# Grouped state products, a parametric ReLU for the sign of the weights, and a one-level last product in a cross-attention and SERF kernel

## The chip, the cores and the metric

The kernel runs on one core of one Trainium2 chip. The metric is the device time of one execution in microseconds. The engines are TensorE (PE in the profile, with its weight loads as PEld), VectorE (DVE), ScalarE (ACT), GpSimd (POOL) and SyncE (SP), which issues most of the DMAs. Each engine works off its own list of instructions in order.

## The reference, cut to what matters

Two blocks follow each other. The first is attention between the tokens `x` of a batch row (8 rows, 8 heads, 512 tokens, 64 columns) and a small state (32 rows a head); the second is a layer with the activation `h * erf(softplus(h))`.

```python
scores = x @ state^T / 8            # per batch row and head
a = exp(scores - max);  a /= sum + 1e-9
xread = a @ state                   # 512 tokens
a2 = the same over state @ x^T / 8
sread = a2 @ x                      # 32 state rows
x2 = concatenate([xread, sread]) with the heads side by side   # 8 * 544 rows of 512
h = x2 @ w_in                       # 512 -> 2048
g = h * erf(softplus(h))
out = g @ w_out                     # 2048 -> 512, 4352 rows in all
```

The weights are handed over as 64-bit floating-point numbers. The kernel computes in 32 bits.

## The kernel before, in words

**Passes and units.** The 2048 hidden columns are worked off in two passes of 1024, since the weights of one pass are what stays on the chip. A unit is one batch row in one pass: unit 0 of the first pass is written out by hand (`first_unit`), units A1 to A7 are the other rows of the first pass, SA and SB are the state rows of both passes, B0 to B7 are the rows of the second pass, whose results are added to what the first pass stored.

**A unit's steps.** `attention` makes the weights `a`, turned, in `y`. `mixed` multiplies a row's state matrices with `w_in` (a 32-row block for each head, on 64 rows of the array), so that the hidden values are `a` times that product; the four blocks X11, X12, X21, X22 and three sums of them (M1 to M4) lie in `m`. `hidden` then forms the product with seven block products instead of eight (the Strassen-Winograd way), in two halves `f0` and `f1`; `chain` spells out the order of the seven and of the copies between them, on banks 0, 1 and 2 of the accumulation memory. Softplus (`soft`), Erf (steps `e0`, `e1`) and the multiplication (`g0`, `g1`) follow on ScalarE and VectorE, in one of two buffers `ring`. `sums_a` prepares the four sums for the second product.

**The second product.** In the first pass and for SA and SB it is `second`: seven products of the one level, steps `p1` to `p7`, in banks 3 to 5, whose results are stored. In the second pass it is `second_twice`: each of the seven is again made of seven (`inner`, with sums of the activations made by `inner_sums` and of the weights made by `twice`). `twice` overwrites the corner `w12` of each of the seven weight blocks with `w22 - w12` (steps t03 to t63). The last unit, B7, has its own form, `second_last`: it reads back what the first pass stored (steps l0 to l3), adds the products to it and stores the sum; two groups of four and two of the seven go through `inner`, and the seventh (S4) is taken at one level, for which `saved` keeps the one corner that it needs.

**Reading the weights.** `piece` turns 1024 64-bit numbers a partition into 32-bit ones, with i0 to i7 for `w_in` and o0 to o7 for `w_out` (i0 in two parts, so there are seventeen): `a0` on ScalarE scales the high words, `a1` on ScalarE scales the low words, `v0` on VectorE shifts the first result left by 3 bits, `v1` adds the low part, `v2` copies the sign bit from the high word. In the profile `a0` is L344, `a1` L346, `v0` L348, `v1` L350, `v2` L351.

**The order.** Nothing is left to a scheduler: `ORDER` is a list of the steps' names, written out, and every engine gets its instructions in that order. A name such as `~7*11` is eleven products of the identity, whose result nobody reads. `issue` calls each step; `in_order` forbids any other order.

**Lines of helpers.** Adds, subtractions and multiplications all have the lines of `add` (L223), `sub` (L224) and `mul` (L225); copies and the DVE's transposes have L231. L575 is a product of `mixed`, L623 of `hidden`, L675 of `second`, L734 of `inner`, L815 and L819 of the last unit's S4 (256 and 128 columns), L854, L865 and L886 of unit 0, L468 the read `sread` of a row, L612 Softplus, L631 Erf, L926 a product of the state units.

In the profile a product is two rows of MATMUL, a transpose one.

Of the kernel before, what the change touches and what calls it, by code (L numbers as in the profile page):

```python
# [8 lines left out]
F32 = mybir.dt.float32  # L9
# [8 lines left out]
lx0 warm lst0 lx1 lx2 lx3 i0l0 lst6 lst3 lst5 lst2 ~7*11 x0 lst4 lst8 s0 lst7 x1 s0c lst1 x0c i1l0  # L18
x3 x1c i1l1 i0l1 q0 x3c i2l1 x2 q00c i2l0 q01c i3l0 x2c tm0 i3l1 i0a0 big0 q1 i0a1 max0 q11c i0v0
q10c less0 ~7*4 tm1 i0v1 u0 exp0 max1 i0v2 u1 less1 o0l0 n00 sum0 exp1 big1 sum1 i1a0 inv0 inv1  # L20
norm0 i1a1 big i1v0 ~6*13 ta0 norm1 i0+a1 i1v1 ~7*1 ta1 i0+a0 wt0 n00c1 i1v2 n00c0 wt1 ta1c i0+v0
~4*6 n02 ta0c i0+v1 n02c0 i2a0 i0+v2 n02c1 o0l1 ~7*5 n01 i2a1 h0 n01c1 a1xq2 i2v0 n01c0 i2v1 a1xq7
h1 wz a1xq6 h0s i2v2 i3a0 a1xq3 u1c ~7*1 n10 i3a1 i3v0 h2 a1xq1 n10c1 h0c i3v1 h1s a1xq4 n10c0 h3
h2s i3v2 a1xq0 h1c o0a0 y01 a1xq5 n12 wn1 o0a1 h4 y02 o1l0 n12c1 wn0 o1l1 h2c n12c0 u0c o2l0 tw1
h4c o0v0 h3s tw0 a1tx3 h3c o0v1 tw1c h5 tw0c h4s o0v2 rd0 a1tx0 h2e rn0 a1tx2 ~7*2 rt0 h7 rc0
a1tx1 h0e y04 h2g yl0 a1s o3l1 h0g a1x2 h5s h6 o2l1 a1c0 a1c1 o3l0 a1tu0 o1a1 i4l0 a1tu1 A1m0 i4l1
a1my0 h6s a1x3 o10 a1mx1 A1m01 a1my1 o1a0 a1mx0 o20 A1m00 a1ms o1v0 h5c a1sb0 h7c h7s o1v1 A1m1
o00 o1v2 a1ex0 A1m11 a1sb1 i5l1 A1m10 o02 a1sm0 a2xq7 a1ex1 A1M1 a1ey1 a1sm1 h6c o12 a1ey0 a1iz
a1nm0 a1ta0 o22 A1M2 h4e a1nm1 o2a1 A1f01 y11 a1ta1 A1f05 A1f0c y12 a1ty1 o2a0 A1f06 A1M3 A1f02
y13 A1f0u2 a1ty0 A1f07 y14 A1f0c11 a1kz o2v0 A1f11 i5l0 A1f0u3 A1M4 a1x0 i4a0 A1f0c22 A1f04 a1iy  # L30
h4g A1f03 A1f0c21 A1f1c o2v1 o3a1 A1f16 A1f0c12 A1f12 A1f1u2 i4v0 a1z3 i4a1 A1f15 a1x1 o2v2 a1z0
A1f17 o3a0 a1z2 i4v1 o24 a1z1 A1f1u3 i5a1 i4v2 A1f14 h6e o3v0 i4k o04 A1f1c22 i6l0 A1f1c11 o3v1
a2xq5 A1f1c21 A1f13 a2xq6 h6g rd1 A1f0s11 a2xq2 y03 A1f0s21 o3v2 o14 a2xq4 i5a0 rn10 rn11 i6l1 rt1
A1f1s11 o06 i5v0 A1f0s12 i5v1 A1f1s22 rc1 o16 o0c i5v2 A1f1s12 A1f1c12 o30 i5k a2tx3 a2xq3 A1f1s21
T1 A1f0s22 a2xq1 o32 a2tx2 a2xq0 T2 A1e1 o34 a2x0 T3 a2x3 a2x1 o36 A1g1 yl1 i6a0 i7l0 A1e0 o26
a2tx1 i6v0 o3c a2tx0 A1g0 a2s a2c1 a2c0 a2tu1 A1p10 o1c a2tu0 i6a1 o1d a2my0 a3xq3 o2c a2mx1 A2m0
A1A1 o3d A1p11 a3xq0 A2m01 a2mx0 A2m00 yk0 a2sb1 A2m1 i7l1 a2sb0 a3xq7 a2ex1 a2my1 A1p50 a2ex0
A1A2 a3xq6 A1pc A2m11 a2sm1 a3xq1 A1p60 A2m10 a2sm0 i6v1 A1p51 a2iz a2nm0 a2nm1 A1p61 a2ta0 i6v2
A2f01 A1pu2 a2ms y21 i6k a2ey0 A1p20 a2ta1 a3xq2 A2f0c A2M1 a2ey1 y22 A2M2 A2f02 a2ty0 A2f06
A2f0c11 a2ty1 A2f05 A2M3 A2f0u2 a2kz y23 A2f11 a2x2 A1A3 a3xq4 A2f07 i7a0 y24 A1p70 a3tx0 A2f0u3  # L40
i7v0 i7a1 A2f0c22 A2f04 A2M4 a2z0 a3tx3 A1p71 A2f0c21 a2z2 A1A4 A2f1c a2z3 a2z1 A2f16 a3tx1 a3xq5
i7v1 A2f03 A2f0s22 o0d A2f1u2 A2f12 i7v2 A1pu3 A2f17 A2f1c11 A2f0c12 o4l0 rd2 A2f1s11 a2iy A1pc22
A2f1u3 A2f0s12 A2f15 A1d3 rn21 rn20 A2f0s11 a3tx2 yl2 rt2 A2f14 A2f1c22 i7k rc2 A2f0s21 T4 yk2 a3s
A2f1c21 o2d A2f1s12 a3x3 A2f13 a3c1 yk1 A2f1s22 A1p21 a4xq0 A2f1c12 a3c0 a3tu1 A2f1s21 a3x1 a3tu0
A1p40 a4xq4 a3mx1 A2e0 a3x2 a3sb1 o4l1 A3m0 a3mx0 a3my1 A1p30 A3m01 A2g0 A3m00 A2e1 A3m1 a3my0
A1p41 A1pc11 A2g1 A1p31 a3ex1 A3m10 a3sb0 A3m11 A2A1 A2p10 a3ex0 A1pc21 a3sm0 a3sm1 A2p11 A1pc12
a3ms a3iz A1d1 a3ey0 a3nm0 A2p50 a4xq1 A2pc a3nm1 a3ey1 a3ta0 a3x0 A2p51 A2A2 a4xq5 a4xq6 y31
a3ta1 A3f01 o4a0 A3M1 A2p60 a3ty0 A3f0c A3M2 y32 A3f02 a3ty1 y33 A3f06 a3kz A3M4 a4xq7 A2p61 A3M3
A3f0u2 a3iy A3f0c11 A2A4 a4xq2 A3f07 A2pu2 y34 a4xq3 o4v0 o4a1 A3f05 A3f11 A3f0u3 a3z0 A3f0c22
A3f04 a3z3 a4tx2 a3z1 A3f03 A3f0s11 a3z2 A3f0c21 A2p20 A3f0c12 A3f1c o4v1 A3f0s12 A3f0s21 A3f16  # L50
A3f0s22 o4v2 A3f12 A3f1u2 A2A3 rd3 o4k A1d0 A3e0 A3f17 yl3 rn30 rn31 a4tx3 o5l1 rt3 A3f15 a4tx0
a4x2 a4tx1 A3f1u3 A2p70 A3f1c11 A3f1c22 rc3 A3g0 a4s A3f1s11 A3f14 a4c0 a5xq5 A3f1s22 A3f13 a4tu0
a4c1 a5xq2 a4mx0 A2p71 A3f1c21 A3f1c12 A3f1s12 A1d2 a4tu1 a5xq0 A3f1s21 A4m0 a4my0 A2pu3 a4x3
a4mx1 A2p21 o5l0 a4my1 a5xq1 A2pc22 A3e1 a4sb0 A2p40 a4x0 a4sb1 A2d3 A4m01 a4x1 A3g1 A2pc11 a5xq4
A2p30 A4m00 o6l0 A4m1 a4ms A3A1 a4ex1 a4ex0 A3p10 a4sm1 a4ey1 a4sm0 A4m10 A4m11 a4iz A2p41 a4nm0
a4ey0 a4ta0 A3p11 a4nm1 A2pc21 A4M1 o5a1 y41 a4ta1 A4f01 a4ty1 A2p31 A4f0c a4ty0 A3pc y42 o5a0
a4kz A4M2 A4f02 a5xq3 A3A2 A4f06 A4f0c11 A4M3 A3p60 A4f0u2 y43 a4iy y44 o5v0 A4f07 o5v1 A4f05
A4f0u3 a4z1 A4M4 a4z2 A4f11 A4f0c22 a4z0 A4f04 A2pc12 a4z3 a5xq6 a5tx1 A4f03 A4f0c21 a5tx0 A3p61
A4f1c a5xq7 a5tx2 A3A3 A2d1 rd4 A4f0s22 A4f0c12 A4f0s12 A4f16 rn41 a5x2 rn40 o5v2 o6l1 rt4 A4f15
A4f1u2 yk3 A4f0s21 a5tx3 A4f17 rc4 a5s A4f1u3 A3pu2 A4f1c22 A4f12 A4f0s11 a6xq1 a5c1 A4f14 a5c0  # L60
a5tu1 a5x1 A4f13 yl4 a5my1 a6xq2 A3p50 a5tu0 A4e0 a5mx1 a6xq3 a5sb1 A5m0 a5mx0 A2d2 A4f1c11 a5x3
a5my0 A3p70 A5m01 a6xq0 a5sb0 A5m00 a5ms A3A4 a5x0 A5m1 o5k a5ex1 a6xq6 A3p71 A4f1c21 a5sm1 a5ex0
a6xq7 A4f1c12 a5ey0 a5sm0 A3p20 A2d0 A5m10 a5iz a6xq5 a5ey1 a5nm0 o6a1 A3p51 a5ta0 y51 A5m11 a5nm1
A5f01 a5ta1 A3p21 A4f1s11 y52 A5M1 A5f0c A4f1s12 A5M2 A3pu3 A5f05 A5M3 A4f1s22 A5f06 a6tx1 a5ty1
A5f02 A5f0u2 a5ty0 A4f1s21 A3p40 A3pc22 a5kz A5f0c11 y53 a6xq4 a6tx0 A5f07 y54 yk4 A4g0 A4e1 A5f11
A3p30 A5f0u3 A4g1 A3pc11 A5f04 a5z0 A3p31 a5z3 A5f0s11 a5iy a5z1 A5M4 a5z2 A3p41 A5f0c22 a6tx2
A5f0c21 A4A1 A5f1c A5f03 A5f0s22 A5f16 a6tx3 o6a0 A3pc12 rd5 A5f1u2 A5f0c12 A3d1 A5f17 yl5 rn51
rn50 o6v0 rt5 A4p10 A5f1u3 A4A3 rc5 A5f0s21 A3pc21 o6v1 a6s A4A2 A5f15 a6c1 a7xq4 a6c0 A5f12
A5f0s12 a6x1 a6tu0 A6m0 a7xq3 a6mx0 a6tu1 A5f14 a6x2 A5e0 a6mx1 A3d3 A4p11 a7xq2 a6sb0 a6my1 A6m00
a7xq6 A4p50 A5f1c22 a6my0 o7l0 a6ex0 a6ms a7xq1 A4A4 A5f13 A4pc A6m01 yk5 A4p60 a6sb1 a7xq5 a6sm0  # L70
a6ex1 a6ey0 a6sm1 a7xq7 A4p61 A5f1c11 a6iz A5f1c21 a7xq0 a6nm0 a6ey1 A6m1 a6ta0 a6x0 A4pu2 a6nm1
A6f01 A6m10 y61 a6ta1 A6m11 A4p70 A6f0c A6M1 y63 a6ty0 A4p71 A6M2 y62 A5f1c12 A4p51 A4pu3 a6iy
# [93 lines left out]
def kernel(  # L166
# [140 lines left out]
    def load_st(h):  # L307
        i, e = h // 2, h % 2
        nc.sync.dma_start(out=st[Ns * i:Ns * i + Ns, 1:B, D * e:D * e + D],
                          in_=state[1:B, h].rearrange("b n d -> n b d"))  # L310

    def piece(kind, j):

        g = j + 4 * (kind == "o") if j < 4 else j
# [741 lines left out]
```

## Time and profile before

| | us |
|---|---|
| median of 3 runs | 714.45 |
| the profiled execution | 714.29 |
| its span, first to last instruction | 712.4 |
| matmuls by line: L675 / L623 / L734 in the chain | 27% / 26% / 24% of the span |
| VectorE, sign bit (L351), 17 operations | 19.6 |
| ScalarE, function table loads, 60 | 77.0 |
| granted TensorE clock | 0.998 |

How to read it: a group's line gives the source line, the engine, the operation, output and inputs, the shape, how often it ran, the busy time and the mean of one; then the idle time of the engine before these instructions and what ended it. In the timeline a line begins with the start and the duration in us. The chain is the work that ended last, followed back from the end.

### The profile page before, as it was taken

To read this page: it belongs to the slowest core of one execution; us is meant where nothing else is said; L and a number is where in the kernel's file an instruction comes from. 1 tells how busy PE (TensorE), PEld (TensorE's weight loads), DVE (VectorE), ACT (ScalarE), POOL (GpSimd) and SP (SyncE) were. 2 spreads that over 40 slices of the span, in tenths; PEclk is the share of its full clock that TensorE was granted. 3 is DMA by queue.
4 is the path that set the end of the run, shared out by engine and by line. 5 is a ranking of instruction groups with operands and counts; after the bars stand their busy time and mean duration, and the time that the engine had idled before them with its cause. 6 is when DMAs were issued, how large, how long until landed. Compare 5 with 4: busy or idle time off the path is not lost.

```text
span 712.4 us, 12455 instructions
## 1 busy us (share of the span) xinstructions
PE 700.4 (98%) x5033; PEld 581.8 (82%) x5033; DVE 554.8 (78%) x749; ACT 468.5 (66%) x706; POOL 37.8 (5%) x38
## 2 busy tenths in 40 slices
PE   8999999999999999999999999999999999999995
PEld 7546468787878787889789879989988998899995
DVE  4999999989979979582644179697959886989894
ACT  2999857869597767634624585667567756695721
POOL 0000000000000000000000002020101111011120
PEclk9999999999999999999999999999999999999999
DMA  9696787759484862642320222124141515141441
GB/s 270 162 288 163 176 221 205 217 145 241 118 219 152 178 185 74 179 158 80 132 75 30 67 75 30 53 28 85 24 89 16 97 16 97 16 68 31 90 60 60
DMA packets 132586, 83.14 MB, mean 117 GB/s; under 512 B 93488, under 2 KB 123696, under 8 KB 132272
## 3 DMA queue, kind: packets, MB, share of 16 engines
q1 hardware_dynamic: 123792, 73.94, 37.0%
q0 software_dynamic: 8192, 7.87, 8.9%
q8 instruction: 40, 0.66, 0.4%
q10 hardware_dynamic: 544, 0.52, 0.2%
q14 instruction: 18, 0.15, 0.1%
HBM read 49.28 MB, written 33.03 MB: 116 GB/s over the span
## 4 chain that ended last, share of the span: by engine, by line
PE 94%; DVE 1%; ACT 0%; issue 0%; DVEq 0%
PE b L675 27%; PE b L623 26%; PE b L734 24%; PE b L575 4%; PE b L886 4%; PE b L926 4%; PE b L865 2%; PE b L468 1%; PE b L494 1%; DVE ring L223 1%; PE b L854 0%; DVE w_in L350 0%; DVE w_in L351 0%; DVE res L223 0%; ACT at L231 0%; PE b L478 0%
## 5 line engine op out<-in xcount | busy, mean ns | idle before, releaser
L675 PE MATMUL b<-ta,ring 128*128 128x256 f32 x840 | 192.2, 380 | 1.1 <-ACT at L231 1.1
L675 PEld LDWEIGHTS b<-ta,ring 128*128 128x128 f32 x840 | 157.6, 190 | 31.8 <-issue 7.5
L231 ACT COPY ring<-b 128x512 f32<-128x512 f32 (+1 forms) x138 | 79.3, 582 | 89.7 <-PE b L623 56.0
L623 PE MATMUL b<-y,m 128*128 128x256 f32 x480 | 122.3, 382 | 0.0
L231 ACT COPY res<-b 128x512 f32<-128x512 f32 (+2 forms) x104 | 54.8, 533 | 86.9 <-PE b L734 43.9
L623 PEld LDWEIGHTS b<-y,m 128*128 128x128 f32 x480 | 87.9, 190 | 17.8 <-issue 3.5
L225 DVE TENSOR_TENSOR ring<-ring 128x2048 f32<-128x2048 f32 (+1 forms) x36 | 77.7, 2166 | 23.1 <-ACT ring L631 23.1
L623 PE MATMUL b<-sy,m 128*128 128x256 f32 x360 | 92.6, 383 | 0.4 <-ACT b L231 0.4
L223 DVE TENSOR_TENSOR ring<-ring,b 128x512 f32<-128x512 f32 (+1 forms) x66 | 44.6, 676 | 51.1 <-PE b L623 17.4
L734 PE MATMUL b<-at,ring 128*128 128x128 f32 x660 | 81.7, 275 | 0.0
L734 PEld LDWEIGHTS b<-at,ring 128*128 128x128 f32 x660 | 79.2, 192 | 2.8 <-ACT b L231 0.8
L612 ACT ACTIVATE ring<-ring 128x512 f32<-128x512 f32 x128 | 77.5, 631 | 2.4 <-DVE ring L223 1.5
L623 PEld LDWEIGHTS b<-sy,m 128*128 128x128 f32 x360 | 65.3, 190 | 15.4 <-issue 4.7
L224 DVE TENSOR_TENSOR ring<-ring 128x1024 f32<-128x1024 f32 (+2 forms) x67 | 75.7, 1134 | 0.3
L651 POOL DMA_DIRECT2D out_dram<-res x32 | 37.1, 1408 | 652.3 <-DVE res L223 572.6
L223 DVE TENSOR_TENSOR res<-res,b 128x512 f32<-128x512 f32 (+2 forms) x50 | 30.6, 612 | 37.9 <-ACT res L231 27.4
L631 ACT ACTIVATE ring<-ring 128x2048 f32<-128x2048 f32 x30 | 57.2, 1911 | 0.2
L231 ACT COPY m<-b 128x512 f32<-128x512 f32 (+2 forms) x65 | 35.3, 565 | 15.1 <-PE b L575 11.5
L231 ACT COPY b<-b 128x512 f32<-128x512 f32 (+2 forms) x57 | 31.2, 551 | 18.7 <-PE b L926 5.5
L231 DVE STREAM_TRANSPOSE at<-at 128x512 f32<-128x512 f32 x56 | 38.0, 696 | 2.9 <-ACT at L231 2.8
L734 PE MATMUL b<-cv,ta 128*128 128x128 f32 x312 | 40.1, 276 | 0.0
L734 PEld LDWEIGHTS b<-cv,ta 128*128 128x128 f32 x312 | 38.0, 192 | 2.1 <-ACT b L231 0.8
(144 smaller groups left out, 906.3 us busy)
## 6 DMA issues: line engine op xcount, KB each, us to landing
out_dram<-res SPq DMA_DIRECT2D x32, 256.0 KB, 2.9
at<-in_x_dram SPq DMA_DIRECT2D x30, 256.0 KB, 4.1
at<-in_x_dram SPq DMA_DIRECT2D x112, 64.0 KB, 2.9
out_dram<-res POOLq DMA_DIRECT2D x28, 256.0 KB, 5.1
cv<-in_moe_w_in_dram SPq DMA_DIRECT2D x12, 512.0 KB, 5.6
cv<-in_moe_w_out_dram SPq DMA_DIRECT2D x12, 512.0 KB, 4.9
kept_y<-y SPq DMA_DIRECT2D x8, 512.0 KB, 5.0
y<-kept_y SPq DMA_DIRECT2D x8, 512.0 KB, 3.8
```

The costliest lines, as they stand in the source:

```text
L223: add = lambda o, a, b: tt(o, a, b, op=ALU.add)
L224: sub = lambda o, a, b: tt(o, a, b, op=ALU.subtract)
L225: mul = lambda o, a, b: tt(o, a, b, op=ALU.mult)
L231: do[name] = lambda: f(*args)
L575: pe.matmul(out=bank[6 + k][Ns * p:Ns * p + Ns, :], lhsT=by, rhs=w_in[r, 4 * j:4 * j + 4, i, :], start=True, stop=True)
L612: act.activation(out=o, in_=i, func=ACTF.Softplus)
L623: pe.matmul(out=to[:, i], lhsT=xs[n - 1][:, q:q + P], rhs=ys[n - 1], start=(start and i == 0), stop=(i == 1), skip_group_check=True)
L631: step(u + "e%d" % o, lambda s=s: act.activation(out=s, in_=s, func=ACTF.Erf))
L651: nc.gpsimd.dma_start(out=to, in_=of, accum_op=ALU.add)
L675: pe.matmul(out=to[:, E2 * h:E2 * h + E2], lhsT=a[:, k // 2, k % 2], rhs=rhs[n][:, k], start=(start and h == 0 and k == 0), stop=(k == 3), ...
L734: pe.matmul(out=out_[:, P * j:P * j + P], lhsT=lhs[:, i], rhs=rhs[:, i], start=(start and j == 0 and i == 0), stop=(i == 1), skip_group_ch ...
L886: pe.matmul(out=bank[3 + r % 3], lhsT=s[:, k, P * r:P * r + P], rhs=wo[0].w[:, k, :], start=(k == 0), stop=(k == NT - 1))
```

## The change

Four things are changed, and the order of all steps is a new one.

`mixed` made the two halves of a unit's state products one after the other, both in banks 6 and 7, with the copies of the first half between them. Now the sixteen products are one step (`m`), the second half in banks 1 and 2, and the copies follow.

In `piece`, `a0` is a parametric ReLU in place of a scaled copy. A positive number is scaled by 2^-112 as before; a negative one by 2^-112 times -2^32, so that it comes out positive with an exponent that is larger by 32. After the shift by 3 bits that part of the exponent is the sign bit. Step `v2` is gone.

The last unit's second product is of one level like `second`, whose products moved to a function of their own, `one_level`; each result is added to what was read back, and stored by halves. For it the seven weight blocks need their corners back: `twice` stores each `w12` in memory before it is overwritten (steps t0k to t6k), and the last unit reads the seven back into place (k0 to k6). `saved` is gone.

`ORDER` has 2257 names instead of 2308, with 32 filler products instead of 43. The built program has 2493 products instead of 2544, 717 VectorE operations instead of 749, 71 loads of a function table instead of 60, and 322 DMAs on SP's queue instead of 305.

```diff
@@ def piece
             step(name + plus + "a0", lambda t=t, hi=hi: act.activation(
-                out=t, in_=hi.bitcast(F32), func=ACTF.Copy, scale=2.0 ** -112))
+                out=t, in_=hi.bitcast(F32), func=ACTF.Prelu, scale=2.0 ** -112,
+                alpha=-2.0 ** 32))
...
-            step(name + plus + "v2", lambda d=d, hi=hi: dve.scalar_tensor_tensor(
-                out=d, in0=hi, scalar=0x80000000, in1=d, op0=ALU.bitwise_and,
-                op1=ALU.bitwise_or))
@@ def mixed
-        for j in range(2):
-            def product(j=j):
+        to = bank[6:8], bank[1:3]
+
+        def product():
+            for j in range(2):
...
-                    pe.matmul(out=bank[6 + k][Ns * p:Ns * p + Ns, :], lhsT=by,
+                    pe.matmul(out=to[j][k][Ns * p:Ns * p + Ns, :], lhsT=by,
                               rhs=w_in[r, 4 * j:4 * j + 4, i, :], start=True, stop=True)
-            step(u + "m%d" % j, product)
+        step(u + "m", product)
+        for j in (1, 0):
             for e in range(2):
-                step(u + "m%d%d" % (j, e), act.copy, X[2 * j + e], bank[6 + e])
+                step(u + "m%d%d" % (j, e), act.copy, X[2 * j + e], to[j][e])
@@ def second_last
+        P_, Q_, R_ = bank[3:6]
         part = ring[1 - slot][:, 0:2].rearrange("p a (k s) -> p (a k) s", s=512)
+        for k, t in enumerate(w.seven()):
+            step(u + "k%d" % k, lambda k=k, t=t: nc.sync.dma_start(out=corner(t), in_=kept_w[k]))
...
-        inner_sums(u + "a", ring[slot], 0, 4)
-        inner_sums(u + "b", ring[slot], 4, 6)
-        inner(u + "a", ws, slot, (0, 3, 4, 5), bank[3:6], res[:, 0:4])
...
-        inner(u + "b", ws, slot, (1, 2), bank[0:3], res[:, 4:6])
...
+        def put_(n, h):
+            nc.sync.dma_start(out=rows_of(b)[:, n // 2 + 2 * h, E2 * (n % 2):E2 * (n % 2) + E2],
+                              in_=part[:, n, E2 * h:E2 * h + E2])
+
+        products = one_level(u, w, slot, 2)
+        u2, u3 = res[:, 0], res[:, 1]
+        halves = [slice(E2 * h, E2 * h + E2) for h in range(2)]
+        products(1, P_, True)
+        step(u + "pc", act.copy, Q_, P_)
+        products(5, R_, True)
+        products(6, Q_, False)
+        step(u + "pu2", act.copy, u2, Q_)
+        step(u + "w2", add, C12, C12, u2)
+        products(2, P_, False)
+        for h, v in enumerate(halves):
+            step(u + "C11%d" % h, add, C11[:, v], C11[:, v], P_[:, v])
+            step(u + "d0%d" % h, put_, 0, h)
+        products(7, Q_, False)
+        step(u + "pu3", act.copy, u3, Q_)
+        step(u + "w5", add, C22, C22, R_)
+        step(u + "C22", add, C22, C22, u3)
...
+        products(4, Q_, False)
+        for h, v in enumerate(halves):
+            step(u + "C21%d" % h, add, C21[:, v], C21[:, v], Q_[:, v])
+            step(u + "d2%d" % h, put_, 2, h)
+        products(3, R_, False)
+        for h, v in enumerate(halves):
+            step(u + "C12%d" % h, add, C12[:, v], C12[:, v], R_[:, v])
+            step(u + "d1%d" % h, put_, 1, h)
+
+    def corner(t):
+        return t.rearrange("p (o i) (c e) -> p o c i e", o=2, c=2)[:, 0, 1]
@@ def twice
-            if k == 6:
-                step("t6c", act.copy, saved, w12)
+            step("t%dk" % k, lambda k=k, w12=w12: nc.sync.dma_start(out=kept_w[k], in_=w12))
```

The piece of the new order that the prediction counts in, from unit 0's first softplus (h0s) on; h and n are its products, tw0 and tw1 transposes, tw0c and tw1c their copies, rd0 the read:

```
h0s n10 wn0 h0c h2 h1s a1xq5 y02 n10c1 h1c n10c0 o1l0 i3a0 h3 o1l1 a1xq6 i3a1 i3v0 h4 a1xq7 h2c i3v1
h2s o2l0 h3s o0a1 o2l1 n12 o3l0 h5 n12c1 h3c o3l1 u0c n12c0 h4c tw0 o0a0 tw1 h4s o0v0 h5s h6 o0v1 tw1c
tw0c i4l1 rd0
```

and the last unit's end, after the first half of product 5:

```
B7p71 B7p51 B7pu3 B7p40 B7w5 B7C111 B7C22 B7d01 B7p41 B7w2 B7C110 B6C12 B7d00 B7p30 B7d31 B6d1 B7C211
B7C210 B7d20 B7d21 B7p31 B7d30 B7C120 B7C121 B7d10 B7d11
```

## The prediction

> **What bounds the kernel now.** I read the page's busy times and the chain that ended last first, because they say whether any engine but TensorE is worth looking at.
>
> ```profile
> span 712.4 us, 12455 instructions
> ...
> PE 700.4 (98%) x5033; PEld 581.8 (82%) x5033; DVE 554.8 (78%) x749; ACT 468.5 (66%) x706; POOL 37.8 (5%) x38
> ...
> PE 94%; DVE 1%; ACT 0%; issue 0%; DVEq 0%
> ```
>
> TensorE works nearly the whole span. So a gain must come out of TensorE's own list, out of the head before it is dense, or out of the tail after it. The chain in order of time gives its prices, and the table by stage says where other engines are close behind it (busy us of each engine in each stretch).
>
> ```profile
> 285.21 10.36 PE b L675 x48
> 457.83 7.14 PE b L734 x64
> ```
> ```profile
> 17.00:27.00 10.00, 9.00 (x96) 7.49 (x93) 9.29 (x21) 8.78 (x15) 0.00 (x0) 1.00 0.58 185
> 27.00:60.00 33.00, 32.91 (x218) 14.35 (x218) 31.29 (x50) 32.26 (x50) 0.00 (x0) 1.00 0.80 222
> 60.00:110.00 50.00, 48.44 (x272) 30.96 (x271) 48.59 (x69) 38.01 (x55) 0.00 (x0) 1.00 0.79 195
> 110.00:712.40 602.40, 595.14 (x4290) 516.33 (x4288) 458.31 (x599) 385.18 (x582) 37.11 (x32) 1.00 0.41 99
> ```
>
> A row of 256 columns costs 10.36/48 = 0.216 us, one of 128 columns 7.14/64 = 0.112; a product is two rows (a transpose is one). After 110 us TensorE is idle for 7.3 us, all of it tail. Between 17 and 27 us VectorE is the full one. Between 27 and 60 us ScalarE is: it rests 0.74 us out of 33. That is the sentence to keep for the ReLU. The timeline there:
>
> ```profile
> 28.62 0.60 ACT L612 ACTIVATE ring<-b 128x512 f32<-128x512 f32 x1
> ...
> 38.54 1.11 ACT L231 COPY at<-b 128x512 f32<-128x512 f32 x2
> ...
> 39.70 0.94 PEld L468 LDWEIGHTS b<-at 128*32 128x32 f32 x64 [0.87 <-ACT at L231]
> ```
> ```profile
> L612 ACT ACT_TABLE_LOAD x26 | 33.4, 1283 | 0.4
> ```
>
> The read of unit 0 (L468) already waits 0.87 us for ScalarE's copies. Last, a group of state products and the tail:
>
> ```profile
> 639.83 0.59 PE L623 MATMUL b<-y,m 128*128 128x256 f32 x2
> ...
> 640.35 1.09 PE L575 MATMUL b<-w_in,st 64*32 64x512 f32 x16
> ...
> 641.37 2.94 PE L734 MATMUL b<-cv,ta 128*128 128x128 f32 x24
> ```
> ```profile
> 704.66 3.09 DVE L223 TENSOR_TENSOR ring<-ring,res 128x512 f32<-128x512 f32 x5
> 704.75 0.39 PE L819 MATMUL b<-sT,ring 128*128 128x128 f32 x2
> ...
> 708.61 0.41 DVE L223 TENSOR_TENSOR ring<-ring,b 128x256 f32<-128x256 f32 x1
> ...
> 709.14 0.46 SPq L827 DMA_DIRECT2D out_dram<-ring  x1
> ```
>
> TensorE ends at 705.1; VectorE then works off its adds until 709.0, and the last store closes the span at 712.4. The profiled execution took 714.3 (1.9 around its span); the runs' median, 714.45, is the same.
>
> **The change, part by part.**
>
> *One group of products for a unit.* The two rows ahead of the group end at 639.83 + 2 x 0.216 = 640.26; the group starts 0.09 later, and the next row 1.02 after that. Its eight products run side by side in two passes of 512 columns, 2 x 0.43 = 0.86. So 0.25 us is entering and leaving. 480 rows are 30 groups; 15 become part of another: at most 3.8 us. I take 0.2 each, 3.0, since each pass still starts its eight products one after another. What it adds is a wait: the second pair of banks is also the chain's, and must be emptied by the unit before, last by a VectorE add (0.68). In the new order at least 1.7 us of matmuls stand between the chain's last product into it and the group, so I cost it at nothing; an add that is one wide operation late (1.2) would cost up to 0.4 in the four tightest units. From 0 to 3.8.
>
> *The ReLU, VectorE's side.* 17 operations of L351 go, 9.7+2.6+2.5+2.4+2.4 = 19.6 us. Three of them (0.68, 0.69, 1.22 = 2.6) stand before the first hidden product, in the stretch where VectorE rests 0.7 us of 10. What is late next is ScalarE, which rests 1.2 there; so I take 1.2, from 0 to 2.6. Between 60 and 110 us VectorE is busy 48.6 of 50 and TensorE loses 1.6; with five more operations gone I take back 1.5, from 0 to 1.6. After 110 us no loss is left to gain.
>
> *The ReLU, ScalarE's side.* The activation itself has the shape of the one it replaces; no row shows it as a ReLU, and I keep 1.16, the row of the old one. But the built program loads a function table 71 times, not 60: Softplus's table does not serve the ReLU. Two of the pieces stand amid unit 0's softplus steps (i3, o0), each with a load before and one after. From that first softplus (28.62) to the end of the copies for the read (39.65) are 11.0 us. The new list has the same seventeen instructions there, two more softplus (1.1 at their spacing) and four loads, 4 x 1.28 = 5.1: 17.2. TensorE meanwhile has one more hidden product (1.7) and two transposing groups (0.8), less a filler of 0.2: 2.3. So the wait grows by 17.2 - 11.0 - 2.3 = 3.9. Below, nothing but the 0.74 of rest could swallow it, or an earlier first softplus; above, seven more loads than before stand ahead of unit 2's first chain product (16 against 9), 9.0.
>
> By the Trainium skill (ScalarE: Activation LUTs, What ACT_TABLE_LOAD costs) a switch costs 2.66 us, a load of 1.283 and a drain of 1.38; the four would then be 10.6 and the total 716.5. The trace agrees on the load and shows no drain, 0.4 us of idle time before 26 loads, so the sum goes by the row.
>
> *The last unit.* Out go 84 products of 128 columns (168 x 0.112 = 18.8), and S4's with the saved corner, 8 rows of 256 and 16 of 128 (1.7 + 1.8): 22.3. In come 56 of 256 columns, 112 x 0.216 = 24.2. TensorE +1.9. In the tail, VectorE's list after the last half of product 5 is ten adds, four of 0.69 and six of 0.42, 5.3 us in all, beside four groups of matmuls of 1.73, 6.9, so it is not behind; after the last product stand a wait of 0.2, an add of 0.41, and the store, 3.3 as now: 3.9 in place of 7.3, so -3.4 (between -3.4 and 0, if VectorE is still behind).
>
> *The corners.* Seven stores and seven loads of 128 KB on SP's queue. The loads are queued among the unit's own reads of the output, with 10.9 us of matmuls or more before each product that needs one, against landings of 2.9 to 3.0. The stores hold VectorE's t*3 steps; the closest has 8.9 us of matmuls between. Behind a late store on SP stand the next unit's y loads. Nothing, unless uncovered (below).
>
> *The rest of the order*: I find no dependency nearer than before and cost it at nothing.
>
> Sum: 714.3 - 3.0 - 1.2 - 1.5 + 3.9 + 1.9 - 3.4 = 711.0.
>
> **The rivals.**
>
> Loads covered: the first softplus comes early enough, or the read is not what TensorE waits for, and the 3.9 vanish: 707.1. For it: ScalarE rests 12 us in 60 to 110. Against: its list is served in order, and the read is in front of everything. 0.25.
>
> Slower than before: ScalarE becomes the bound until unit 2. All seven extra loads are paid, 9.0 in place of 3.9, and the 1.5 are not won: 717.6. It decides once ScalarE's rest between 27 and 110 us is used up by waits that it cannot reorder. 0.14.
>
> The stall slows TensorE's clock. The span begins so:
>
> ```profile
> 0.78 3.75 PE L371 MATMUL b<-const-float32-1.0 128*128 128x128 f32 x16 [0.78 <-PEq L1042]
> ...
> 4.33 3.33 PE L371 MATMUL b<-ident 128*128 128x128 f32 x22
> ```
>
> The first sixteen rows of 128 columns took 3.75 us, 0.234 each against 0.112, and the next 22 still 0.151: about 5.6 us at half pace, 2.8 lost. If the long wait brings that back once: 713.8. TensorE's longest idle time here is 1.1, so the trace does not test it. 0.08. The Trainium skill (TensorE: Matmul & The Clock Gate, Part 1) has a rule for this: an idle window of about 3.4 us brings the slow clock back.
>
> Stores uncovered: each t*3 waits a whole landing, 7 x 2.9 = 20.3: 731.3. 0.06. Against: the distances above.
>
> Everything won and more, under 700: 0.02; no row holds that much.
>
> **How the numbers follow.** The forecast has 0.45. The range: down to the covered case with the larger group gain (-0.8) and the whole of VectorE's 2.6 (-1.4), 705; up to the ScalarE-bound case, 718. It leaves out the uncovered stores, the under-700 case and some edges of the rest. Two per cent, about what a measurement of this kernel can tell from no change, is 14.3 us: faster is 0.02, slower the uncovered stores, 0.06, the rest 0.92.
>
> **What would show it.** Fifteen L575-like groups of 32 rows, each about 2.0 us; a wait of 4 to 5 us ahead of unit 0's read, put down to ScalarE's copies, with four loads in the list before it; TensorE ending at about 705 and the span 3.9 later. A read that waits under a microsecond, or TensorE's idle time spread over units 1 and 2, would make me wrong about where; a tail over 5 us, or stalls before the inner sums' products, about the end.

## The result, and the profile after

The changed kernel takes 710.95 us (median of 6 runs, 710.65 to 711.42) against 713.74 for the kernel before on the same chip: a ratio of 0.9961, with an interval of 0.9947 to 0.9974. The forecast was 711.0. The profiled execution has a span of 708.9, 3.56 less than before. The total is right; how far its parts are is the subject of the rest.

The page of the kernel after, its busy times, the engines' shares of the chain of waits, and the function-table loads of the line with most of them (count, busy us and mean ns, idle time ahead of them):

```profile
span 708.9 us, 12281 instructions
...
PE 695.3 (98%) x4931; PEld 582.1 (82%) x4931; DVE 524.4 (74%) x717; ACT 481.0 (68%) x709; POOL 37.7 (5%) x38
...
PE 91%; ACT 4%; DMA 1%; issue 0%; DVE 0%; SPq 0%; DVEq 0%; ACTq 0%
...
L611 ACT ACT_TABLE_LOAD x31 | 39.8, 1283 | 0.5
```

In the chain ScalarE had 0% before and has 4% now. The table by stage tells where (stretch, its length, busy us and instructions of PE, PEld, DVE, ACT and POOL, granted clock, DMA share, GB/s):

```profile
17.00:27.00 10.00, 9.02 (x76) 5.77 (x75) 9.62 (x22) 9.35 (x17) 0.00 (x0) 1.00 0.82 235
27.00:60.00 33.00, 27.66 (x176) 12.74 (x175) 20.16 (x31) 32.45 (x42) 0.00 (x0) 0.95 0.65 170
60.00:110.00 50.00, 49.82 (x303) 31.25 (x302) 46.51 (x75) 44.89 (x66) 0.00 (x0) 1.00 0.74 180
```

Between 27 and 60 us TensorE is busy 27.66 us where it was 32.91, VectorE 20.16 where it was 31.29, and ScalarE is full as before. ScalarE's part of the timeline there (start, duration, line; L342 is the ReLU, L611 Softplus, L878 Erf):

```profile
30.16 1.28 ACT L342 ACT_TABLE_LOAD   x1
31.45 1.15 ACT L342 ACTIVATE w_in<-ring 128x1024 f32<-128x1024 f32 x1
...
34.12 1.28 ACT L611 ACT_TABLE_LOAD   x1
...
38.14 0.62 ACT L230 COPY ring<-b 128x512 f32<-128x512 f32 x1
38.76 1.28 ACT L342 ACT_TABLE_LOAD   x1
40.06 1.14 ACT L342 ACTIVATE ta<-cv 128x1024 f32<-128x1024 f32 x1
41.21 1.28 ACT L611 ACT_TABLE_LOAD   x1
...
43.48 1.08 ACT L230 COPY at<-b 128x512 f32<-128x512 f32 x2
```

These are the four loads that the prediction counts, two around each of the pieces i3 and o0. A load begins when the copy before it ends (38.14 + 0.62 = 38.76) and the ReLU begins 0.02 after the load: no further stop is seen beside its 1.28. What goes besides is the overlap that neighbours without a load have (the two copies at 43.48 take 1.08 together, the one at 38.14 takes 0.62). TensorE meanwhile, with the wait and what ended it in brackets:

```profile
34.96 0.67 PE L852 MATMUL b<-w_in,st 64*32 64x256 f32 x16 [1.15 <-DVE w_in L349]
36.07 1.98 PE L863 MATMUL b<-y,m 128*128 128x512 f32 x4 [0.44 <-ACT ring L611]
38.32 1.09 PE L405 MATMUL b<-ident,ring 128*128 128x128 f32 x8 [0.27 <-ACT m L230]
39.25 1.88 PE L863 MATMUL b<-y,m 128*128 128x512 f32 x4
44.61 1.94 PE L464 MATMUL b<-at 128*32 128x64 f32 x64 [3.48 <-ACT at L230]
46.48 2.10 PE L863 MATMUL b<-y,m 128*128 128x512 f32 x3
```

The matmuls of unit 0's read (L464) wait 3.48 us for ScalarE's copies. The 0.87 of the kernel before is no match for this number: it is idle time of the weight loads (PEld). The weight loads now wait 4.31:

```profile
44.61 1.70 PEld L464 LDWEIGHTS b<-at 128*32 128x32 f32 x64 [4.31 <-ACT at L230]
```

The matmuls of the read in the kernel before waited for nothing (a wait would stand in brackets):

```profile
39.70 1.10 PE L468 MATMUL b<-at 128*32 128x64 f32 x64
```

So the wait grew by 3.4 us in the weight loads and by 3.5 in the matmuls. Three more waits stand ahead of it, of 1.15, 0.44 and 0.27. The first is put down to VectorE's last step on piece i3, which itself stands behind the ReLU of that piece; but 0.98 of it is there without that ReLU too (the run with two copies below). And the read takes 1.94 us for 64 rows: the clock is at half speed there.

A unit's group of state products, now of 32 rows, and the end of the span:

```profile
642.01 1.95 PE L573 MATMUL b<-w_in,st 64*32 64x512 f32 x32
643.89 1.60 PE L738 MATMUL b<-cv,ring 128*128 128x128 f32 x12
```

```profile
699.16 7.14 SPq L795 DMA_DIRECT2D out_dram<-ring  x8
...
705.02 0.75 DVE L222 TENSOR_TENSOR ring<-ring,b 128x256 f32<-128x256 f32 x2 [2.70 <-PE b L672]
```

VectorE has waited 2.70 us when the last product is done, so it isn't behind; TensorE ends at about 705.0 and the span 3.9 after it, as forecast.

Where the time went can be followed in one more way. For each row of TensorE's list I take the time at which it starts less what the rows before it need back to back (0.216 us for 256 columns, 0.112 for 128, 0.430 for 512, for rows on a part of the array about the pace inside their groups; fillers left out): what TensorE has lost so far. Worked out from the traces, in us:

| lost by | 27 us | 50 | 110 | 160 | 680 | span after the last row's start |
|---|---|---|---|---|---|---|
| before | 19.8 | 22.7 | 26.7 | 28.0 | 37.8 | 7.58 |
| after | 17.7 | 25.6 | 27.9 | 30.7 | 35.9 | 4.28 |

From 27 to 50 us the changed kernel loses 7.9 where the old one lost 2.9. It has won 2.1 ahead of that, wins 1.7 back until 110 and 3.1 between 110 and 680, in spite of 1.5 more lost from 110 to 160. With 1.85 more of work and 3.3 less behind the last row that is -2.1 + 5.0 - 1.7 - 3.1 + 1.85 - 3.3 = -3.35, and -3.56 by the spans (the rest is TensorE's last 30 us and rounding).

### The profile page after: what moved, and what is told of

The parts are those of the page before. It is cut to its first block, busy times and chain, and to the rows that moved or that the text cites. A ratio compares the mean times of both kernels' runs of the same rounds, so it can differ in the third digit from the quotient of the medians.

```text
span 708.9 us, 12281 instructions
## 1 busy us (share of the span) xinstructions
PE 695.3 (98%) x4931; PEld 582.1 (82%) x4931; DVE 524.4 (74%) x717; ACT 481.0 (68%) x709; POOL 37.7 (5%) x38
## 4 chain that ended last, share of the span: by engine, by line
PE 91%; ACT 4%; DMA 1%; issue 0%; DVE 0%; SPq 0%; DVEq 0%; ACTq 0%
PE b L672 31%; PE b L622 26%; PE b L738 22%; PE b L573 4%; PE b L924 4%; PE b L884 2%; PE b L464 1%; PE b L490 1%; DMA at<-in_x_dram 1%; ACT ring L611 1%; ACT L611 1%; ACT ring L345 0%; ACT L342 0%; ACT ring L230 0%; PE b L863 0%
## 5 line engine op out<-in xcount | busy, mean ns | idle before, releaser
L672 PE MATMUL b<-ta,ring 128*128 128x256 f32 x840 | 189.8, 380 | 0.0
L622 PE MATMUL b<-y,m 128*128 128x256 f32 x480 | 121.4, 382 | 1.4 <-ACT ring L230 1.2
L622 PEld LDWEIGHTS b<-y,m 128*128 128x128 f32 x480 | 88.0, 190 | 17.3 <-issue 3.5
L230 ACT COPY res<-b 128x512 f32<-128x512 f32 (+2 forms) x98 | 52.1, 537 | 71.1 <-PE b L672 35.2
L222 DVE TENSOR_TENSOR ring<-ring,b 128x512 f32<-128x512 f32 (+1 forms) x71 | 46.7, 661 | 67.9 <-PE b L622 25.1
L622 PE MATMUL b<-sy,m 128*128 128x256 f32 x360 | 90.9, 380 | 0.0
L611 ACT ACTIVATE ring<-ring 128x512 f32<-128x512 f32 x128 | 76.4, 629 | 5.3 <-DVE ring L222 5.0
L622 PEld LDWEIGHTS b<-sy,m 128*128 128x128 f32 x360 | 65.7, 190 | 10.2 <-issue 1.3
L223 DVE TENSOR_TENSOR ring<-ring 128x1024 f32<-128x1024 f32 (+2 forms) x65 | 73.2, 1137 | 0.3
L738 PE MATMUL b<-at,ring 128*128 128x128 f32 x588 | 73.0, 275 | 0.0
L738 PEld LDWEIGHTS b<-at,ring 128*128 128x128 f32 x588 | 71.4, 192 | 1.6
L222 DVE TENSOR_TENSOR res<-res,b 128x512 f32<-128x512 f32 (+2 forms) x46 | 28.5, 619 | 53.6 <-ACT res L230 27.9
L672 PE MATMUL b<-at,ring 128*128 128x256 f32 x168 | 37.7, 380 | 0.0
```

What stands on the lines that cost most here:

```text
L222: add = lambda o, a, b: tt(o, a, b, op=ALU.add)
L223: sub = lambda o, a, b: tt(o, a, b, op=ALU.subtract)
L230: do[name] = lambda: f(*args)
L611: act.activation(out=o, in_=i, func=ACTF.Softplus)
L622: pe.matmul(out=to[:, i], lhsT=xs[n - 1][:, q:q + P], rhs=ys[n - 1], start=(start and i == 0), stop=(i == 1), skip_group_check=True)
L672: pe.matmul(out=to[:, E2 * h:E2 * h + E2], lhsT=a[:, k // 2, k % 2], rhs=rhs[n][:, k], start=(start and h == 0 and k == 0), stop=(k == 3), ...
```

## The experiments

Each run of several is the median against the kernel before on the same chip; the changed kernel's ratio of 0.9961 is what to hold them against. Where a part is only some tenths of a microsecond the profiled spans are compared, and said so. A single span carries a chance of its own: TensorE's first rows run at about half pace, and how long they do differs. The fourteen filler rows that start at 4.33 us in the changed kernel take 2.84 us; in the run with two groups, where they start at 4.14, they take 1.73, and the rows behind them start 1.3 us earlier.

**The groups of state products.** The state products of a unit are put back into two groups, one matmul step apart:

```diff
@@ def mixed
-        def product():
-            for j in range(2):
...
+        def product(j):
...
-        step(u + "m", product)
+        for j in range(2):
+            step(u + "m" if j == 0 else u + "mm", product, j)
@@ ORDER, for unit A3
-... A1p41 a3ex1 ...
+... A1p41 A3mm a3ex1 ...
```

> The changed kernel with each unit's state products in two groups again, the second group one matmul step behind the first (15 units). Theory (entering and leaving a group costs TensorE 0.25 us): +3.8, 714.7, between 714.0 and 715.0, with 30 groups of 16 rows at about 1.1 us between them and TensorE otherwise as before. Rival (the cost of a group is hidden in TensorE's queue, the gain came from the order): 711 to 712.

Measured: 717.74, ratio 1.0051 (1.0038 to 1.0063), a span of 714.2, 5.3 longer than the changed kernel's. By the medians it is 6.8, beyond the range on record; the profiled execution is the fastest of its five (715.97 to 718.59). TensorE's timeline of the changed kernel, and then of this run, at the same unit:

```profile
125.64 5.34 PE L672 MATMUL b<-ta,ring 128*128 128x256 f32 x24
130.91 1.95 PE L573 MATMUL b<-w_in,st 64*32 64x512 f32 x32
132.79 1.56 PE L672 MATMUL b<-ta,ring 128*128 128x256 f32 x6
```

```profile
129.70 1.09 PE L567 MATMUL b<-w_in,st 64*32 64x512 f32 x16
130.72 1.99 PE L667 MATMUL b<-ta,ring 128*128 128x256 f32 x8
132.64 1.09 PE L567 MATMUL b<-w_in,st 64*32 64x512 f32 x16
133.66 0.70 PE L667 MATMUL b<-ta,ring 128*128 128x256 f32 x2
```

Eight rows of 256 columns between the two groups take from 130.72 to 132.64, 1.92, and not 8 x 0.216 = 1.73. Row by row: the first row of a group starts 0.093 late, the first row behind a group 0.089, and the second row behind a group 0.104 once more; inside a group 0.07 is lost whatever its length. That is 0.356 a group, and fifteen groups fewer are 5.3 us. The spacing is the same at 29 of the 30 groups. That the spans differ by 5.3 too is partly chance: some units of this run lose another 1.7 between them, and 1.7 are won ahead of 60 us, 1.3 of them in the first 8 us (the fillers just told of). So the mechanism stands, and its size is 5.3 by the rows, beyond the 3.8 that the theory held for the most.

**The loads amid unit 0's softplus steps.** Pieces i3 and o0 are converted as before, the other fifteen stay ReLUs:

```diff
@@ def piece
-            step(name + plus + "a0", lambda t=t, hi=hi: act.activation(
+            relu = not (name in ('i3', 'o0'))
+            step(name + plus + "a0", lambda t=t, hi=hi, relu=relu: act.activation(
                 out=t, in_=hi.bitcast(F32), func=ACTF.Prelu, scale=2.0 ** -112,
-                alpha=-2.0 ** 32))
+                alpha=-2.0 ** 32) if relu else act.activation(
+                out=t, in_=hi.bitcast(F32), func=ACTF.Copy, scale=2.0 ** -112))
...
+            if not relu:
+                step(name + plus + "v2", ...)
```

> The changed kernel with two pieces of the weights, i3 and o0, converted as before: a plain copy on ScalarE and a sign step on VectorE; the four function-table loads amid unit 0's softplus steps go with that, two VectorE steps (2 x 1.2 us) come back. Theory (the loads stand in front of unit 0's read): the read's wait falls from 3.48 us to under 1, TensorE's clock stays at full speed, 710.95 - 3.5 - 1.4 = 706.1, from 705.5 to 707.5. Rival (ScalarE holds TensorE up until 110 us anyway, and what is won at the read is lost again behind it): the wait falls, the stalls between 60 and 160 us grow by as much, 709.5 to 711.5. Rival (the two VectorE steps are what the stage lacks): slower than 711.5.

Measured: 704.45, ratio 0.9869 (0.9854 to 0.9884); a span of 703.3, 5.6 shorter than the changed kernel's. TensorE's timeline of this run:

```profile
34.44 0.67 PE L852 MATMUL b<-w_in,st 64*32 64x256 f32 x16 [0.98 <-DVE w_in L347]
35.04 1.98 PE L863 MATMUL b<-y,m 128*128 128x512 f32 x4
36.86 1.04 PE L405 MATMUL b<-ident,ring 128*128 128x128 f32 x8
37.73 1.88 PE L863 MATMUL b<-y,m 128*128 128x512 f32 x4
39.55 1.10 PE L464 MATMUL b<-at 128*32 128x64 f32 x64
```

The read starts at 39.55 in place of 44.61 and waits for nothing, and the clock stays up. Nothing of it is lost again behind: the read starts 5.07 earlier and the last row 5.56. Of this 0.35 is there at 8 us, where the edit does nothing, so by the rows the two pieces cost 5.2. The waits of 0.44 and 0.27 ahead of the read are gone as well; the one at L852 is still 0.98, now for the sign step that came back (L347). The loads are on the path, and the time falls below the theory's range: 6.5 under the changed kernel's by the medians, where the read's wait and the slow clock behind it were put at 4.9.

The same two pieces as ReLUs in the kernel before, in its own order, all else as it was:

```diff
+            relu = name in ("i3", "o0")
...
-i3v2 ... o0v2
```

> The kernel before in its own order, with a ReLU in place of copy and sign step for the two pieces i3 and o0 alone: four loads amid unit 0's softplus steps, two sign steps of 1.2 us less. The prediction's term for these loads (+3.9, measured against this order): 714.2 + 3.9 = 718.1, from 717.0 to 719.0, with the read's wait at 3 us or more. Rival (5.6, as the changed kernel loses by the same two pieces): 719.8, from 719.1 to 721. Rival (TensorE gets it back by 110 us, since the stage waits for VectorE there): 714 to 716.

Measured: 719.1, ratio 1.0069 (1.0056 to 1.0082), 4.9 slower, and nothing of it comes back: the read starts 4.9 later and so does the last row. The time lies between the two sizes on record. The expected wait isn't there, though. The timeline of this run:

```profile
40.73 0.66 PE L408 MATMUL b<-ident,ring 128*128 128x128 f32 x4 [1.80 <-ACT m L226]
41.23 1.88 PE L864 MATMUL b<-y,m 128*128 128x512 f32 x4
44.57 1.10 PE L467 MATMUL b<-at 128*32 128x64 f32 x64 [1.46 <-ACT at L226]
```

The delay is spread over several waits for ScalarE, of which the read's is one of 1.46. A late engine is met wherever the waiting engine next needs it, and the sum of these waits is what counts.

A third piece, i7, whose ReLU stands amid softplus steps of unit 3, is taken out of the ReLUs as well (the diff is against the run with i3 and o0 as copies):

```diff
-            relu = not (name in ('i3', 'o0'))
+            relu = not (name in ('i3', 'o0', 'i7'))
```

> The run with i3 and o0 converted by copy and sign step, and a third piece, i7, too: its ReLU stands amid softplus steps of unit 3 and costs two loads shortly before TensorE waits 1.2 us for ScalarE. Theory: that wait goes, 704.45 - 1.2 = 703.2, from 702.6 to 703.8. Rival (the sign step of 1.2 us on VectorE, or the next wait, takes it back): 704.1 to 704.9.

Measured: 703.62, ratio 0.9848 (0.9835 to 0.9862), the fastest of all; its span is 2.3 shorter than that of the run with two, its median 0.8. The changed kernel and the run with two have this wait, which is gone here (the view of waits of the changed kernel: engine, line, what it waited for, us in total, times, longest):

```profile
PE b L464 <- ACT at L230: 3.5, 1, 3.5
PE b L852 <- DVE w_in L349: 1.7, 2, 1.1
PE b L622 <- ACT ring L230: 1.2, 1, 1.2
```

The median lies in the theory's range, and the intervals of the two runs overlap; that the wait at L622 goes is shown, and the rows there come 1.3 earlier for it (0.7 of the 2.3 is there at 8 us already); that it is worth 1.2 in the median is not shown.

**The clock.** Fillers are put in front of the read, in the time in which TensorE waits:

```diff
-tw1c tw0c i4l1 rd0
+tw1c tw0c i4l1 ~3*14 rd0
```

> The changed kernel with 14 matmuls of 128 columns whose result nobody reads (1.6 us) put in front of unit 0's read, in the time in which TensorE waits for ScalarE's copies; nothing else is changed. Theory (the 3.48 us of idle time bring a slow clock, which costs 1.4 us after it): TensorE's idle stretch falls to about 1.9 us, the granted clock stays 1.0, the read takes 1.1 us and not 1.94, 709.5, between 709.0 and 710.2. Rival (what the slow clock costs is swallowed by the next wait for ScalarE): the read is fast and the total stays 710.6 to 711.3.

Measured: 709.96, ratio 0.9947 (0.9935 to 0.9960). A product is two rows, which the expectation overlooked: 28 rows of 3.29 us filled the wait but for 0.36. The read took 1.10 and the clock stayed up. But the span is only 0.38 shorter than the changed kernel's: TensorE is 1.40 ahead when unit 0's next products are done, then waits 0.50 for a sum of VectorE's and a little more, and keeps 0.35. So the slow clock did cost time, 0.4 in that execution at most (0.1 of it is there at 8 us); the medians differ by 1.0 with intervals that overlap, so the size isn't settled between the two. The granted clock of the changed kernel's six executions is 0.998 in two and 0.994 in four, and 1.0 in all five with the fillers, so more time at the slow clock than the trace has may lie in the medians; that is not shown.

What brings it is told by the windows of 3.41 us into which the granted clock falls. First the changed kernel, then the run with two groups, then the first of the runs with the old last unit (below):

```profile
40.79:44.20 3.41, 0.34 (x1) 0.00 (x0) 2.94 (x4) 3.38 (x6) 0.00 (x0) 1.00 1.00 408
44.20:47.61 3.41, 3.00 (x66) 2.31 (x67) 1.12 (x3) 3.38 (x4) 0.00 (x0) 0.50 0.59 185
```

```profile
38.06:41.47 3.41, 1.77 (x5) 0.47 (x3) 1.52 (x2) 3.37 (x4) 0.00 (x0) 1.00 0.95 372
41.47:44.88 3.41, 1.58 (x66) 1.25 (x67) 1.90 (x4) 3.38 (x6) 0.00 (x0) 1.00 0.95 336
44.88:48.30 3.42, 2.92 (x8) 1.19 (x7) 2.44 (x4) 3.42 (x5) 0.00 (x0) 1.00 0.06 18
```

```profile
692.18:695.59 3.41, 1.35 (x12) 1.38 (x13) 3.02 (x4) 0.18 (x1) 1.66 (x2) 1.00 0.99 125
695.59:699.00 3.41, 3.41 (x19) 3.41 (x18) 1.62 (x3) 1.26 (x3) 0.00 (x0) 0.50 0.68 106
```

The run with two groups has the same wait, 3.47 us, and keeps its clock, because the wait falls into two windows in which TensorE is busy for 1.77 and 1.58. In the changed kernel it falls into one, with 0.34 busy, and the next window runs at half speed. The third kernel lost the clock behind a wait of 2.17 in a window with 1.35 busy. The second run with the old last unit (below) has the changed kernel's list up to here and the same wait of 3.48. Its windows lie so that TensorE is busy for 1.29 us in the one that holds the wait's first 2.1 us, and the clock is at half speed for the two windows after it, 6.83 us from 42.38 on. Counted from the row before the read, it falls 1.2 us behind the changed kernel in that stretch. Against the run with the fillers the changed kernel keeps 0.2 us of what the clock took, and this run 1.5.

**VectorE's side of the ReLU.** All seventeen pieces are converted as before, in the changed kernel's order, each sign step right behind its v1 (the diff is against the run with i3 and o0 as copies):

```diff
-            relu = not (name in ('i3', 'o0'))
+            relu = not (True)
```

> The changed kernel in its own order with all 17 conversions as before, copy and sign step; 19.6 us of VectorE work come back, 11 table loads go. Theory, by the terms of the prediction: -3.5 and -1.4 at the read, up to -1.4 for the stall at 154 us, +1.2 to +2.6 in front of the first hidden product, +1.5 between 60 and 110 us: 707.4 to 709.3, most likely 708.3. Rival (VectorE's relief is the larger part of the change, in this order of steps): 711 to 714.

Measured: 711.62, ratio 0.9973 (0.9964 to 0.9983): the rival. Against the run in which only i3 and o0 are copies it has fifteen more sign steps and four loads fewer (around i7 and o7), and a span that is 6.2 longer. TensorE's list is the same in both, so the loss can be read row by row: 2.8 are there by 49 us, although the start is 0.7 ahead (part of it a slow clock from 24.85 on), 5.4 by 106, 6.5 by 132; 1.5 come back where the wait behind i7's loads is gone; 1.4 more are lost until 260. So the ReLU of these fifteen is worth 6.2 in this order, and the ReLU as a whole, loads and all, only 0.6 by the spans (709.5 to 708.9), or 1.7 from 8 us on, since the run with seventeen copies is 1.1 ahead there.

The other way round: the kernel before, in its own order, with all seventeen ReLUs.

```diff
-                out=t, in_=hi.bitcast(F32), func=ACTF.Copy, scale=2.0 ** -112))
+                out=t, in_=hi.bitcast(F32), func=ACTF.Prelu, scale=2.0 ** -112,
+                alpha=-2.0 ** 32))
...
-            step(name + plus + "v2", ...)
```

> The kernel before, in its own order, with only the conversions changed: ReLU on ScalarE, no sign steps on VectorE (17 steps, 19.6 us). In the changed kernel's order the runs with copies give about 5.6 us for the loads amid unit 0's softplus steps and 6.2 us for the other pieces' sign steps. Theory (both sizes belong to the edit and not to the order): 713.8 + 5.6 - 6.2 = 713.2, from 711.5 to 714.5. Rival (the prediction's sizes, loads 3.9 and relief 2.7, hold in the old order): 715.0, from 714.5 to 716.5. In both the wait in front of unit 0's read grows to 3 us or more.

Measured: 721.95, ratio 1.0108 (1.0095 to 1.0122), 7.7 slower: both theories fall. Between 27 and 50 us it loses 4.4 more than the kernel before, about as with i3 and o0 alone (4.2). But the other fifteen, which bring 6.2 in the new order, cost 2.9 in the old one (spans of 720.2 and 717.3). One place shows how. ScalarE's, VectorE's and TensorE's timelines of this run (L339 is the ReLU, L504 the Exp of unit 1's attention, L226 on VectorE a transpose):

```profile
52.00 1.28 ACT L339 ACT_TABLE_LOAD   x1
53.30 1.12 ACT L339 ACTIVATE ta<-cv 128x1024 f32<-128x1024 f32 x1
...
59.08 0.63 ACT L504 ACTIVATE at<-at 128x512 f32<-128x512 f32 x1
```

```profile
59.74 0.69 DVE L507 TENSOR_REDUCE z<-at 128x16 f32<-128x512 f32 x1 [2.26 <-ACT at L504]
...
63.35 0.71 DVE L226 STREAM_TRANSPOSE y<-at 128x512 f32<-128x512 f32 x1
```

```profile
64.21 1.10 PE L616 MATMUL b<-y,m 128*128 128x256 f32 x4 [1.11 <-DVE y L226]
```

A ReLU with its load stands ahead of the Exp in ScalarE's list; VectorE has nothing to do for 2.26 us until that comes; and TensorE waits 1.11 for VectorE's transpose at the end of the sequence. The run with i3 and o0 alone has neither wait. VectorE is named as the last to be late, but it had 5.7 us less to do than before between 60 and 110 us (42.92 for 48.59); the delay is ScalarE's.

**The last unit.** The second product of B7 in its old two-level form, spliced in at that product's start:

```diff
@@ def second_last (body of before), def twice
-            step("t%dk" % k, ...)
+            if k == 6:
+                step("t6c", act.copy, saved, w12)
@@ ORDER: the kernel before's from B7p10 on
```

> The changed kernel with the last unit's second product by two levels again: 84 products of 128 columns, a saved corner of the weights, no stores or loads of corners, and the old order from that product on. Theory (by the prediction's terms: TensorE -1.9, tail +3.4): 712.5, from 711.9 to 713.1, with TensorE ending 1.9 us earlier and the span 7.3 after it. Rival (the new form saves nothing, because VectorE is never behind in either tail or the corners' transfers cost something on the way): 710.0 to 711.3.

Measured: 718.05, ratio 1.0052 (1.0039 to 1.0064). The trace puts the excess on the splice: the sums of the inner products (VectorE's) came too late, three gaps of 4.5 us in all by the rows' starts, and the slow clock shown above. Neither time on record was met. Taken up from the middle of the hidden products (step B7f1c) instead:

> The changed kernel with the last unit's second product by two levels, as in the first such run, but with the old order taken up earlier, from the middle of the last unit's hidden products, so that the sums of its inner products stand beside products of the unit before. Of the first run's 7.1 us, its trace puts 4.5 on waits for these sums and some 1.7 on a slow clock behind the longest wait. Theory (both came from where that run was spliced): they go, 712.5, from 711.7 to 713.3. Rival (the two-level form costs more at this place in any order): 714.5 or more.

Measured: 713.14, ratio 0.9984 (0.9972 to 0.9995): inside the theory's range, 2.2 slower than the changed kernel by the medians (its nine executions lie between 711.36 and 714.28), 3.0 by the spans, of which 0.7 is one wait left in the splice. By the table's method TensorE's work is 1.85 less, the end behind the last row's start 7.58 in place of 4.28, and 1.6 more are lost on the way, with the 0.7 of the splice in it and 0.4 that are lost ahead of 50 us, where the edit does nothing and the clock was slow for two windows. So the new form is worth 3.0 - 0.7 - 0.4 = 1.9 in these two executions, against 1.5 in the prediction.

**The order alone.** All three edits undone, in the changed kernel's order, first with the late splice and then with the early one:

```diff
@@ piece, mixed, second_last, twice: as in the three runs above
@@ ORDER: the changed kernel's, with v2 behind each v1, mm one product behind each m
```

> The changed kernel's order with all three edits undone: copies and sign steps, state products in two groups, the last unit by two levels. Its work is the kernel before's; what is left of the change is the order (and 71 less 11 table loads). Theory (the parts add up: +0.6 for the conversions, +5.4 for the groups, +1.5 for the last unit on 710.95): 718.5, from 717.3 to 719.5, so that the order by itself would cost the old work 4 to 5 us. Rival (the order is neutral for the old work, and the parts do not add up): 713.0 to 715.0.

> All three edits undone in the changed kernel's order, with the same earlier splice for the last unit. Theory (the parts add up, and the order alone costs the old work about 4 us): 718.5, from 717.3 to 719.5. Rival (the excess of the first such run was all splice): 713.5 to 715.0.

Measured: 724.1, ratio 1.0144 (1.0127 to 1.0160), with the same two longest waits of 2.2 and 1.3 in the splice; and 719.77, ratio 1.0087 (1.0073 to 1.0101), with the early one. The second does the old kernel's work in the new order, and is 5.6 slower for it. The steps that come back stand right behind each v1 and one product behind each m; other places for them were not tried, so 5.6 is the price of the new order with the old steps at these places. And the parts add up: undoing the groups, the conversions and the last unit one at a time costs 5.3, 0.6 and 3.0 in the spans, and 708.9 + 8.9 = 717.8; measured with all three undone, 718.0. That they agree to 0.2 is partly luck, since each of these spans carries about a microsecond of chance; by the medians the sum is 710.95 + 6.8 + 0.7 + 2.2 = 720.6 against 719.77, which lies just above the range on record.

The table once more, for the runs that bear on it:

| lost by | 27 us | 50 | 110 | 160 | 680 |
|---|---|---|---|---|---|
| before | 19.8 | 22.7 | 26.7 | 28.0 | 37.8 |
| old work, new order | 19.6 | 22.4 | 27.4 | 30.3 | 43.4 |
| seventeen ReLUs, old order | 18.5 | 25.8 | 33.6 | 34.8 | 45.6 |
| after | 17.7 | 25.6 | 27.9 | 30.7 | 35.9 |
| after, i3, o0, i7 as copies | 16.6 | 19.4 | 21.3 | 23.3 | 28.0 |

The old work in the new order loses 0.7 more than before until 110 us, 1.6 more from there to 160, and 3.3 more in the 520 us after that, 0.4 of it in the splice. Which steps lose the rest was not followed further.

## Why the prediction was right, and where it was not

The total was right within 0.1 us of the median, and the mechanism of one stage as well: ScalarE's loads stand before the read of unit 0, and TensorE waits for them there. The prediction counts from 714.3, and the kernel before took 713.74 on the chip of the comparison: 3.3 less was forecast, and 2.8 less was measured (3.56 by the spans). The parts were off by up to 2.3 us, in both directions, and the order, put at nothing, by more.

- *One group of products*, -3.0 with 3.8 for the most: it is -5.3. The step "0.25 us is entering and leaving" measured from the row before the group to the row behind it. The second row behind a group is late by another 0.104, in the trace of before too, and was not looked at. The wait that the merged group might add, costed at nothing, isn't there: no L573 stands in the view of waits.
- *VectorE's relief in the head*, -1.2: the table gives -2.1, within its bounds (0.2 of it is there for the old work in the new order).
- *VectorE's relief until 110 us*, -1.5: the table gives -1.7 from 50 us on, about 0.4 of which is one group less (two in that stretch, where there were three). In the new order, bringing the sign steps back costs 2.6 between 50 and 106 us.
- *"After 110 us no loss is left to gain"*: wrong as it stands. The loss of the old kernel there is mostly in the groups (26 of 0.356, 9.3 of the 11.1 us until 680), but in the new order the sign steps, when they are brought back, cost 2.6 behind 106 us. That stage also has a wait of 1.2 for ScalarE, behind two loads that the prediction had given no price.
- *The loads*, +3.9: the stage from 27 to 50 us loses 5.0 more, i3 and o0 alone cost 4.9 in the old order and 5.6 in the new (5.2 from 8 us on). The count of four loads and the place were right, and so, nearly, was the list: 17.2 us were forecast from the first softplus to the end of the copies, and the trace has 16.75 (27.81 to 44.56). "The wait grows by 3.9" was half a microsecond too much: like for like it grew by 3.4 (0.87 to 4.31 in the weight loads). The reading that the read "already waits 0.87 us" was wrong, since the matmuls did not wait. What the term left out is the rest of what the loads cost: waits of 0.44 and 0.27 ahead of the read, and the slow clock behind it. ScalarE's list has to be compared with every wait on the way. By the rule of the Trainium skill that the prediction weighed (ScalarE: Activation LUTs, What ACT_TABLE_LOAD costs), four switches would be 10.6, an estimate from its figures; the trace has 0.02 between a load and its function and no drain, and the runs 4.9 to 5.6.
- *The last unit*, +1.9 and -3.4: +1.85 and -3.3, and about 0.5 more won among the products in the one execution compared.
- *The rest of the order*, nothing: for the old work it costs 5.6. With the ReLUs it gains about 3.0 (an estimate: the new order with ReLUs, two groups and the old last unit would be at 708.9 + 5.3 + 3.0 = 717.2, and the old order with ReLUs measured 720.2). This is the step that failed. The prediction took the new order as neutral and priced each edit from the trace of the old one; the runs show that price and order can't be parted. In the old order the ReLU costs 7.7, in the new one it gains 0.6 by the spans; and the new order without the edits is slower than the old one. Why the old work loses in the new order behind 110 us stays open.

That 711.0 came out is therefore largely luck. By edits the prediction has -3.0 for the groups, +1.2 for the ReLU, -1.5 for the last unit and nothing for the order; by the spans the runs have -5.3, -0.6, -3.0 (1.1 of it splice and clock) and +5.6.

The rivals: the loads were not covered. ScalarE wasn't the bound until unit 2, though one wait of 1.2 between 110 and 160 us is for it. The clock did fall in the profiled execution, which was put at 0.08, at a price of 0.4 and not 2.8: the whole stretch at half speed is 3.4 us, and three quarters of what it took came back at the next wait. In another execution of the same list, with 6.83 us at half speed, the price was 1.5. The Trainium skill (TensorE: Matmul & The Clock Gate, Part 1) has the slow clock behind an idle window of about 3.4 us, and the windows run freely, wherever the kernel starts. That the phase of the window decides, the pair of runs with waits of 3.48 and 3.47 shows; that the window must be idle, they do not: it had 0.34, 1.35 and 1.29 us of work in the cases above. The corners' stores held nobody up: in the changed kernel no wait for them stands in the view of waits.

## What to carry to other kernels

An edit's price holds for the order of work that it was read in: ask which engine each wait of the *new* order is for before calling an engine's relief a gain, and try the edit alone and the order alone, since neither may win by itself. A function that the neighbours' table doesn't hold should stand where the table already fits, or be done piece by piece in the cheaper way: three pieces of seventeen taken out of the ReLU won more than the whole change (7.3 us by the medians against 2.8). And when a group of unlike instructions is priced, follow the rows behind it until they are back at their own pace.

## What was not expected of the hardware

A group of matmuls on 64 rows and 32 columns of the array, among those on 128 by 128, costs 0.356 us beyond its rows: 0.093 before its first row, 0.07 inside, 0.089 behind it, and 0.104 at the second row behind it, which looks like any other. Sixteen or thirty-two rows make no difference.

The granted clock fell to 0.5 for one window of 3.41 us after windows in which TensorE was busy for 0.34 and 1.35 us, for two after one with 1.29, and stayed at 1.0 after one with 1.58. Three traces with the same list of work up to the same wait have no slow window, one and two, by where the windows lie. The clock came back after a slow window with 3.00 us of work and not after one with 2.06. Busy time doesn't settle it alone: in the run with seventeen copies it fell after a window with 1.66, part of it matmuls on 64 rows.

```profile
21.43:24.85 3.42, 1.66 (x36) 0.92 (x36) 3.26 (x5) 1.47 (x3) 0.00 (x0) 1.00 0.66 249
24.85:28.26 3.41, 3.41 (x12) 1.51 (x5) 3.29 (x8) 3.26 (x7) 0.00 (x0) 0.50 0.87 211
```

What is counted in a window stays open.
